# Shifting four attention operand tiles by 64 bytes in on-chip memory

## The chip, the cores and the metric

The kernel runs on one core of one Trainium2 chip. The metric is the device time of one execution in microseconds (us), and the time given for a kernel is the median of its runs. A profiled execution of the kernel before took 845.1 us; the span of its instructions is 843.3 us, and the remaining 1.8 us lie around the span.

## The reference

Two mixers run on the same sequence `x` of 2048 rows by 512 columns in float32, and a gate per row mixes their results.

```python
g = sigmoid((x * gate_w).sum(-1, keepdims=True))
# A: a Fourier layer, the real part of a transform along both axes
a  = x @ dft_hid_re.T;  b = x @ dft_hid_im.T
y  = dft_seq_re @ a - dft_seq_im @ b
# B: attention, 32 heads of 16, each query sees itself and the 255 keys before it
q, k, v = split(x @ wqkv)
p  = softmax(where(0 <= i - j < 256, q @ k.T * 16**-0.5, -1e9))
out = g * y + (1 - g) * ((p @ v) @ wo)
```

## The kernel before, in words

**Two streams on TensorE.** The attention (B) is worked off as 128 steps: four groups of eight heads, and in each group 32 blocks of 64 queries. A step has four parts `p`, each of which holds two heads, stacked as 128 rows of the array. `s_pair` multiplies a block of queries with a window of up to 320 keys and takes the row maximum; `t_pair` runs 19 steps later (`LAG`) and computes the transposed scores with the maximum folded in, for one block of keys and up to 320 queries. Between two such attention matmuls the function `fill` puts dense matmuls of 512 columns: the projections, then the Fourier layer's products over the sequence (`c_part`, line 529). In most of the attention this gives a steady order on TensorE: one attention matmul, two dense ones, one attention matmul, two dense ones. The order of all engines but GpSimd is written out by hand.

**The tiles in question.** `ring[0]` and `ring[1]` hold the queries and the keys of the running groups (128 partitions, four parts of 2048 float32 each). A matmul of `s_pair` or `t_pair` streams a window of a ring past stationary weights, and these weights are a *pad*: `pads[i][b]` is a tile of four parts by 128 columns, in which `make_pad` writes a block of the ring twice, masked by a column `half` of ones and zeros, so that two heads stay apart. There are four pads: `i` is 0 for the queries of `s_pair` and 1 for the keys of `t_pair`, and `b` alternates from step to step. VectorE writes three of the four halves of a step (line 350) and ScalarE one (line 348). So each of the 1024 attention matmuls (512 at line 367, 512 at line 449) has one weight load of 128 columns from a pad.

**Where tiles lie.** A partition of on-chip memory is a row of bytes, and the tiles of the pool `const` lie one behind another in the order in which they are first asked for. Before them stand 1,152 bytes of other things. All sizes per partition are multiples of 128 bytes but those of the small 64-byte columns, so each small tile that is asked for moves everything behind it by 64 bytes. In the kernel before, the order and the start addresses are:

| tile | starts at byte | modulo 128 |
|---|---|---|
| four pads of 2048 bytes | 1152, 3200, 5248, 7296 | 0 |
| two rings of 32768 bytes | 9344, 42112 | 0 |
| `mask`, `ident` | 74880, 76160 | 0 |
| `half` (64 bytes) | 76672 | 0 |
| `vpad` twice | 76736, 78784 | 64 |
| `gl`, `g1`, `g0` (64 bytes each) | 80832, 80896, 80960 | 64, 0, 64 |
| `home` | 81024 | 0 |
| `big`, `hi`, `lo`, `raw`, `ev`, `pt`, `sm` and the rest | from 93376 on | 64 |

The dense matmuls take both operands from `big`, `hi` and `lo`, all at 64 modulo 128. Near the end the products with `wo` (line 922) take both operands from spots in the rings that begin 16 elements, which is 64 bytes, past a multiple of 128 bytes. The pads' memory is used again there: `wo_fetch` and `first_load` put tiles with the pads' tags in it.

Of the kernel before, what the change touches and what calls it, by code (L numbers as in the profile page):

```python
# [7 lines left out]
F32 = mybir.dt.float32  # L8
# [6 lines left out]
P = 128  # L15
# [17 lines left out]
def fnet_window_mix(ctx: ExitStack, tc: tile.TileContext, xT, x, wqk, wv, wr, wi, cr, ci, wo, gw, out):  # L33
    nc = tc.nc

    const = ctx.enter_context(tc.tile_pool(name="const", bufs=1))
# [21 lines left out]
    def f(ap):  # L58
        return ap.bitcast(F32)
# [4 lines left out]
    def mark(e, ins):  # L64
        last[e] = ins.ins

    @contextmanager
    def behind(*engines):
        with ExitStack() as es:
            for e in engines:  # L70
                if e in last:
                    es.enter_context(tc.issue_after(last[e]))
            yield
# [91 lines left out]


    NPAD = 2
    pads = [[const.tile([P, NP, P], F32R, name=f"pad{i}_{b}") for b in range(NPAD)] for i in range(2)]
    ring = [const.tile([P, NP, S], F32R, name=f"ring{i}") for i in range(2)]

    mask = const.tile([P, WIN], F32, name="mask")
# [9 lines left out]
    mark("pool", nc.gpsimd.affine_select(ident[:], f(ident[:]), pattern=[[1, P]], compare_op=OP.is_equal, fill=0.0,  # L181
                                         base=0, channel_multiplier=-1))

    cols = const.tile([P, 16], F32, name="half")
    half, side = cols[:, :2], cols[:, 2:4]
    mrow = cols[:, 4:6]
    for h in range(2):
# [10 lines left out]
    def clear_rows(i, ss):  # L198
        with behind("pool"):
            mark("pool", nc.gpsimd.memset(f(ring[i][96:128, :, ss * 512:(ss + 1) * 512]), 0.0))  # L200
# [4 lines left out]
    for ss in range(4):  # L205
        for i in (1, 0):
            clear_rows(i, ss)
    vpad = [const.tile([P, 4, NP, 32], F32, name=f"vpad{b}") for b in range(2)]

    def clear_pads():  # L210
# [7 lines left out]
                                         mask[96:128, :256].rearrange("r (p c) -> r p c", p=NP),  # L218
                                         AF.Identity, bias=mrow[96:128, h:h + 1], scale=0.0)

    gl = const.tile([P, 16], F32, name="gl")
    g1 = const.tile([P, 16], F32, name="g1")
    g0 = const.tile([P, 16], F32, name="g0")
    gwb = []

# [112 lines left out]
    def make_pad(i, n):  # L338
        if not 0 <= n < NG * NB:
            return  # L340
        t = pads[i][n % NPAD]
        b = n % NB
        with behind(*(("act", "dve") if n < NPAD else ("dve",) if i == 0 and n < 24 else ())):
            for h in range(2):
# [768 lines left out]
```

## Time and profile before

| | value |
|---|---|
| median of 3 runs (lowest, highest) | 845.56 us (845.48, 846.09) |
| profiled execution, its span | 845.1 us, 843.3 us |
| granted TensorE clock | 1.00 |
| TensorE matmul busy (instructions) | 838.5 us, 99% (5310) |
| TensorE weight load busy | 695.8 us, 83% (5310) |
| VectorE busy | 643.8 us, 76% |
| ScalarE busy | 611.1 us, 72% |
| GpSimd busy | 298.8 us, 35% |
| DMA | 161.03 MB, mean 191 GB/s |

A matmul's entry in the profile lasts from the start of its streaming to the modelled end of its results, and the next matmul starts while it is still draining. So a sum of such durations is no sum of time; what one matmul costs is the distance from its start to the next one's start, and this is read from the timeline. The weight load of the next matmul runs while the one before it streams.

### The profile page before, as it was taken

What the parts mean: (1) busy time and instruction counts of PE and PEld (TensorE: products, weight loads), DVE (VectorE), ACT (ScalarE), POOL (GpSimd) and SP (SyncE); (2) the same over time, 40 slices, a digit from 0 to 9 for tenths busy, and PEclk for the clock granted to TensorE, in tenths of its full rate; (3) what the DMA queues carried; (4) which work ended last, traced back from release to release, by engine and by line L of the source; (5) the groups of instructions that cost most, each with busy time, mean ns of one, the idle gap of its engine ahead of it and who ended that gap; (6) DMA issues with size and microseconds to landing.
All of it is one profiled execution on the core that took longest, in us unless ns stands there. A gap on an engine that the chain in (4) does not pass through costs nothing.

```text
span 843.3 us, 17171 instructions
## 1 busy us (share of the span) xinstructions
PE 838.5 (99%) x5310; PEld 695.8 (83%) x5310; DVE 643.8 (76%) x2083; ACT 611.1 (72%) x1832; POOL 298.8 (35%) x606
## 2 busy tenths in 40 slices
PE   9999999999999999999999999999999999999998
PEld 7888888888888888888888887878887878878997
DVE  5588978677979787787877877878987867666874
ACT  6488888878888897787877977867777865553430
POOL 8102333233232233342333243343242357756410
PEclk9999999999999999999999999999999999999999
DMA  8776678485766173534454547979874256455732
GB/s 295 251 227 187 217 243 283 159 259 202 220 222 189 54 232 107 177 120 121 140 160 126 168 153 223 298 214 309 274 216 149 96 179 198 137 192 196 220 133 92
DMA packets 94475, 161.03 MB, mean 191 GB/s; under 512 B 26800, under 2 KB 35504, under 8 KB 94384
## 3 DMA queue, kind: packets, MB, share of 16 engines
q1 hardware_dynamic: 93952, 159.28, 59.1%
q8 instruction: 42, 0.69, 0.3%
q10 hardware_dynamic: 432, 0.66, 0.2%
q14 instruction: 49, 0.40, 0.1%
HBM read 108.27 MB, written 51.64 MB: 190 GB/s over the span
## 4 chain that ended last, share of the span: by engine, by line
PE 99%; DVE 1%; issue 0%; ACT 0%; DVEq 0%; ACTq 0%
PE dc L529 42%; PE dab L304 11%; PE dqk L281 10%; PE t L449 9%; PE s L367 8%; PE o L475 8%; PE dv L304 5%; PE t L922 5%; PE s L269 1%; PE dv L593 0%; PE s L387 0%; DVE pad L350 0%; PE t L559 0%; DVE sm L369 0%; ACT sm L372 0%
## 5 line engine op out<-in xcount | busy, mean ns | idle before, releaser
L529 PE MATMUL dc<-big,hi 128*128 128x512 f32 x1020 | 344.7, 393 | 0.0
L369 DVE CUSTOM_DVE_ANT_0 sm<-s,mask 128x320 f32<-128x320 f32 (+4 forms) x512 | 235.5, 465 | 111.4 <-PE s L367 71.2
L372 ACT ACTIVATE sm<-sm,ml 128x320 f32<-128x320 f32 (+4 forms) x512 | 278.2, 544 | 56.4 <-DVE ml L369 52.1
L450 ACT ACTIVATE pt<-t 128x320 f32<-128x320 f32 (+4 forms) x392 | 159.5, 411 | 83.4 <-PE t L449 78.1
L529 PE MATMUL dc<-big,lo 128*128 128x512 f32 x510 | 200.2, 393 | 0.0
L529 PEld LDWEIGHTS dc<-big,hi 128*128 128x128 f32 x1020 | 179.3, 188 | 21.4
L454 POOL TENSOR_SCALAR_AFFINE_SELECT pt<-pt 128x128 f32<-128x128 f32 x196 | 77.1, 393 | 275.0 <-ACT pt L450 273.7
L449 PE MATMUL t<-ring,pad 128*128 128x320 f32 (+4 forms) x512 | 156.8, 306 | 0.0
L367 PE MATMUL s<-ring,pad 128*128 128x320 f32 (+4 forms) x512 | 154.9, 303 | 0.1
L350 DVE TENSOR_SCALAR pad<-ring,half 96x256 fp32r<-96x256 f32 x384 | 120.0, 359 | 5.4 <-PE t L449 4.9
L449 PEld LDWEIGHTS t<-ring,pad 128*128 128x128 f32 x512 | 96.1, 188 | 30.9 <-issue 8.7
L367 PEld LDWEIGHTS s<-ring,pad 128*128 128x128 f32 x512 | 96.2, 188 | 20.6 <-DVE ml L369 0.7
L529 PEld LDWEIGHTS dc<-big,lo 128*128 128x128 f32 x510 | 95.9, 188 | 12.0
L372 ACT ACTIVATION_READ_ACCUMULATOR sm<-sm,ml 128x1 f32 x512 | 98.1, 192 | 0.0
L588 DVE TENSOR_TENSOR lo<-raw,hi 128x512 fp32r<-128x512 f32 x137 | 94.3, 696 | 2.7 <-ACT hi L588 2.5
L304 PE MATMUL dab<-hi,big 128*128 128x512 f32 x256 | 88.9, 394 | 0.0
L281 PE MATMUL dqk<-big,hi 128*128 128x512 f32 x240 | 85.0, 393 | 0.0
L432 POOL TENSOR_SCALAR vpad<-vr,half 128x256 f32<-128x256 f32 x64 | 62.2, 983 | 62.1 <-PE o L475 29.5
L348 ACT ACTIVATE pad<-ring,half 96x256 fp32r<-96x256 f32 x128 | 66.9, 522 | 0.0
L454 POOL TENSOR_SCALAR_AFFINE_SELECT home<-home 128x128 f32<-128x128 f32 x60 | 33.8, 564 | 90.2 <-ACT home L450 85.7
L458 POOL TENSOR_SCALAR_AFFINE_SELECT pt<-pt 128x128 f32<-128x128 f32 x172 | 62.9, 366 | 0.0
L588 DVE CAST hi<-raw 128x512 fp32r<-128x512 f32 x126 | 54.3, 437 | 11.3 <-PE dc L529 10.6
(122 smaller groups left out, 1034.2 us busy)
## 6 DMA issues: line engine op xcount, KB each, us to landing
qk_scr<-home SPq DMA_DIRECT2D x32, 512.0 KB
ring<-qk_scr SPq DMA_DIRECT2D x32, 512.0 KB
raw<-cr SPq DMA_DIRECT2D x32, 512.0 KB
raw<-ci SPq DMA_DIRECT2D x32, 512.0 KB
r_scr<-ev SPq DMA_DIRECT2D x42, 256.0 KB
ab_scr<-home SPq DMA_DIRECT2D x20, 512.0 KB
big<-ab_scr SPq DMA_DIRECT2D x20, 512.0 KB
ring<-qk_scr SPq DMA_DIRECT2D x32, 256.0 KB
```

The source lines that it names most:

```text
L281: nc.tensor.matmul(ps, w[a][:, c:c + 128], XT[dk, ss][:, b], start=n == 0, stop=n == 11)
L304: nc.tensor.matmul(ps, XT[dk, ss][:, a, c * 128:(c + 1) * 128], wh[b], start=n == 0, stop=n == 11)
L350: mark(f"pad{i}", nc.vector.tensor_scalar(dst, src, half[:96, h:h + 1], None, op0=OP.mult))
L367: nc.tensor.matmul(ps[:, :w], PAD[0, n][:, p], ring[1][:, p, k0:k0 + w], start=True, stop=True)
L369: mark("dve", nc.vector.tensor_tensor_reduce(out=sm[:, :w], in0=ps[:, :w], in1=mask[:, WIN - w:], scale=1.0, scalar=3e38, op0=OP.add, op1= ...
L372: mark("act", nc.scalar.activation(sm[:, :w], sm[:, :w], AF.Exp, bias=nm[:, c], scale=-1.0, accum_out=l[:, c]))
L449: nc.tensor.matmul(ps[:, :w], PAD[1, n][:, p], ring[0][:, p, q0:q0 + w], start=True, stop=True)
L450: nc.scalar.activation(pt[:, p, :w], ps[:, :w], AF.Exp, scale=-1.0)
L454: nc.gpsimd.affine_select(a, a, pattern=[[0, 2], [2, 64]], compare_op=OP.is_ge, fill=0.0, base=1, channel_multiplier=-1)
L475: nc.tensor.matmul(OT[g, sb][32 * p:32 * p + 32, q - sb * 512:e - sb * 512], v2[:, p], pt[:, p, q - q0:e - q0], start=first, stop=kb == 8 ...
L529: nc.tensor.matmul(ps, w[a][:, i % 8 * 128:i % 8 * 128 + 128], ab[SC[i]][:, b], start=i == ends[0] and a + b == 0, stop=i == ends[1] and a ...
L588: return fn(*args)
```

## The change

Three 64-byte tiles are asked for at other places of the program; nothing that any instruction computes changes. `half` now comes ahead of the pads, `gl` between the pads and the rings, and `g1` ahead of `vpad`.

```diff
     NPAD = 2
+    cols = const.tile([P, 16], F32, name="half")
     pads = [[const.tile([P, NP, P], F32R, name=f"pad{i}_{b}") for b in range(NPAD)] for i in range(2)]
+    gl = const.tile([P, 16], F32, name="gl")
     ring = [const.tile([P, NP, S], F32R, name=f"ring{i}") for i in range(2)]
...
-    cols = const.tile([P, 16], F32, name="half")
     half, side = cols[:, :2], cols[:, 2:4]
...
     for ss in range(4):
         for i in (1, 0):
             clear_rows(i, ss)
+    g1 = const.tile([P, 16], F32, name="g1")
     vpad = [const.tile([P, 4, NP, 32], F32, name=f"vpad{b}") for b in range(2)]
...
-    gl = const.tile([P, 16], F32, name="gl")
-    g1 = const.tile([P, 16], F32, name="g1")
     g0 = const.tile([P, 16], F32, name="g0")
```

By the sizes, the pads then start at 1216, 3264, 5312 and 7360, which is 64 modulo 128. The two 64-byte tiles together move the rings by 128 bytes, to 9472 and 42240, which is again 0 modulo 128; `mask`, `ident` and `vpad` move by 128 bytes as well, and `g0`, `home` and all that follows stay where they were.

## The prediction, as put on record

> **What bounds the kernel now.** I read the page first. TensorE is busy for the whole span, at full granted clock, and the chain of waits runs almost only through it.
>
> ```profile
> span 843.3 us, 17171 instructions
> PE 838.5 (99%) x5310; PEld 695.8 (83%) x5310; DVE 643.8 (76%) x2083; ACT 611.1 (72%) x1832; POOL 298.8 (35%) x606
> PE 99%; DVE 1%; issue 0%; ACT 0%; DVEq 0%; ACTq 0%
> ```
>
> So a change shows in the time only if it alters the distance between two matmul starts, or makes TensorE wait. Second view: the waits in front of weight loads, where a late pad would stand.
>
> ```profile
> PEld t L449 <- issue: 8.7, 20, 0.5
> PEld o L475 <- issue: 5.3, 15, 0.4
> ```
>
> These are its two largest entries (total us, times, longest), and no entry names the pad writers at lines 348 and 350. Third, the timeline of TensorE in a steady stretch (start, duration), where each attention matmul is followed by two dense ones:
>
> ```profile
> 362.51 0.31 PE L367 MATMUL s<-ring,pad 128*128 128x320 f32 x1
> 362.65 0.39 PE L529 MATMUL dc<-big,lo 128*128 128x512 f32 x1
> 362.88 0.39 PE L529 MATMUL dc<-big,hi 128*128 128x512 f32 x1
> 363.11 0.31 PE L449 MATMUL t<-ring,pad 128*128 128x320 f32 x1
> ...
> 379.91 0.31 PE L449 MATMUL t<-ring,pad 128*128 128x320 f32 x1
> ...
> 617.14 0.31 PE L449 MATMUL t<-ring,pad 128*128 128x320 f32 x1
> ...
> 641.67 0.31 PE L449 MATMUL t<-ring,pad 128*128 128x320 f32 x1
> ```
>
> From 362.51 to 379.91 the timeline holds 29 such stretches of three matmuls, so one takes 17.40 / 29 = 600 ns. From 617.14 to 641.67 it holds 40, so one takes 24.53 / 40 = 613 ns. The same operands at the same places modulo 128 run in two steady states, 13 ns apart. What sets the state I cannot read.
>
> **The change: what it touches.** Counts come from the groups by shape:
>
> ```profile
> L449 PEld LDWEIGHTS t<-ring,pad 128*128 128x128 f32 x512 | 96.1, 188 | 30.9 <-issue 8.7 <-DVE ml L369 0.8 <-DVE ev L496 0.5
> L367 PEld LDWEIGHTS s<-ring,pad 128*128 128x128 f32 x512 | 96.2, 188 | 20.6 <-DVE ml L369 0.7 <-ACT pt L450 0.4
> L529 PEld LDWEIGHTS dc<-big,hi 128*128 128x128 f32 x1020 | 179.3, 188 | 21.4
> L350 DVE TENSOR_SCALAR pad<-ring,half 96x256 fp32r<-96x256 f32 x384 | 120.0, 359 | 5.4 <-PE t L449 4.9 <-DVE ml L369 0.2
> L348 ACT ACTIVATE pad<-ring,half 96x256 fp32r<-96x256 f32 x128 | 66.9, 522 | 0.0
> ```
>
> No instruction, wait or queue entry is added or removed. 1,024 weight loads read from 64 instead of 0 modulo 128, and 512 writes go there. Rings, mask and `vpad` keep their place modulo 128.
>
> **(a) The load itself.** A pad's load at 0 modulo 128 takes 188 ns and a dense one at 64 takes 188 ns. I take 0 for the load's own time.
>
> **(b) The load beside the streaming matmul.** A pad's load runs beside the dense matmul before the attention matmul. Before, the stream is at 64 and the load at 0; after, both are at 64, as for a dense load beside a dense matmul. What that pairing costs shows late, where three dense matmuls follow each attention matmul:
>
> ```profile
> 717.08 0.31 PE L449 MATMUL t<-ring,pad 128*128 128x320 f32 x1
> 717.23 0.62 PE L529 MATMUL dc<-big,hi 128*128 128x512 f32 x2
> 717.68 0.39 PE L529 MATMUL dc<-big,lo 128*128 128x512 f32 x1
> 717.91 0.31 PE L449 MATMUL t<-ring,pad 128*128 128x320 f32 x1
> ...
> 722.87 0.31 PE L449 MATMUL t<-ring,pad 128*128 128x320 f32 x1
> ```
>
> From 717.08 to 722.87 lie seven stretches, 5.79 / 7 = 827 ns each. Against 600 ns the third dense matmul, whose stream is beside a dense load, costs 827 - 600 = 227 ns. In the rows at 362, the dense matmul beside a pad's load goes from 362.88 to 363.11, 230 ns, in steps of 10. In the seven late stretches it takes on average 224 ns (from 717.68 to 717.91 and six alike), and the two before it 228 each (717.23 to 717.68 and six alike). So the pairing that is coming costs between 3 ns less and 4 ns more than the one that goes, and my value is 0: 227 lies between 224 and 230. Times 1,024 this is -3.1 to +4.1 us, with 0 as forecast.
>
> **A rule beside this.** The Trainium skill, page "SBUF — State Buffer", section "Who interferes with whom", gives TensorE two independent read ports, one for the moving operand and one for weight loads; by it the address of a load cannot touch the stream. The trace agrees to the 4 ns above; it shows only these pairings.
>
> **(c) The attention matmul's own stream** keeps 0 modulo 128, and the load beside it is a dense one, as before: 0. That the class does not tell is seen where both exist in one width, 256:
>
> ```profile
> L922 PE MATMUL t<-ring 128*128 128x256 f32 x312 | 39.9, 283 | 0.0
> L367 PE MATMUL s<-ring,pad 128*128 128x256 f32 x16 | 4.5, 281 | 0.0
> ```
>
> Line 922 has both operands at 64, line 367 both at 0: 283 against 281 ns, which is 2 ns on a modelled duration.
>
> **(d) Writing the pads.** No row writes a pad at 64, so I take the same line or operation with its output in `home` (0) and in a tile at 64:
>
> ```profile
> L450 ACT ACTIVATE pt<-t 128x320 f32<-128x320 f32 x344 | 145.4, 427 | 68.2 <-PE t L449 63.3 <-PE s L367 3.9
> L450 ACT ACTIVATE home<-t 128x320 f32<-128x320 f32 x104 | 44.2, 425 | 7.0 <-PE t L449 5.9 <-POOL home L454 0.4
> L90 DVE TENSOR_TENSOR home<-dqk,home 128x512 fp32r<-128x512 f32 x15 | 10.2, 683 | 1.4 <-ACT home L88 1.4
> L90 DVE TENSOR_TENSOR big<-dab,big 128x512 fp32r<-128x512 f32 x12 | 8.2, 685 | 1.0 <-ACT big L88 1.0
> ```
>
> ScalarE: 427 at 64 and 425 at 0. VectorE: 685 and 683. So a pad write may take 2 ns more: 384 x 2 = 0.8 us on VectorE and 128 x 2 = 0.3 us on ScalarE, over the whole span, hidden under TensorE. The cover:
>
> ```profile
> 300.00:400.00 100.00, 100.00 (x677) 83.24 (x676) 76.68 (x272) 79.73 (x248) 33.22 (x82) 1.00 0.50 151
> ```
>
> The third and fourth busy columns behind the length are VectorE and ScalarE. A step of the attention is eight stretches, 4.8 us, so 100 us hold 21 steps and 63 of VectorE's pad writes; it idles 23.3 us there, 0.37 us for each write. The write would have to double before VectorE became the bound, and then all of the excess would be on the path. I take 0.
>
> **(e) The end.** `wo_fetch` and `first_load` use the pads' memory, so those loads and VectorE's and ScalarE's reads of them move too. (d) prices that at 2 ns an operation, and there are some tens: below 0.1 us.
>
> **The sum.** 0 + 0 + 0 + 0 + 0, so the profiled execution stays at 845.1 us (843.3 of span and 1.8 around it). The median of the three runs is 0.5 us above that, so I put the median at 845.6 us. About 0.2% of it, 1.7 us, is what a measurement of this kernel can tell from no change.
>
> **Rivals.**
>
> *Slower: the like pairing disturbs.* Stream and load at 64 modulo 128 side by side cost more than 64 beside 0, at each of the 1,024 dense matmuls ahead of an attention matmul. For it: the 228 against 224 ns in the late rows. Against: the last dense matmul differs from the others also in what follows it, and its next distance starts from a ring. At 4 ns it adds 4.1 us: 849.7. It shows from 1.7 us / 1,024 = 1.7 ns a load on. Its far form is that each stretch which now takes 600 ns goes to 613: by the starts in the timeline 540 stretches of two dense matmuls keep to 600 or within 3 ns, so 540 x 13.3 = 7.2 us, 852.8.
>
> *Faster: the long state goes.* If the mixture of loads at 0 and at 64 lets the order fall into the 613 ns state, loads all at 64 may keep it out. By the same count 155 stretches of two dense matmuls are one step longer, the forty above among them; 155 x 13.3 = 2.1 us: 843.5. Against: the state comes and goes with the same operands, and the rings stay at 0.
>
> *Much faster: each pad load costs the stream something now.* Between 512 and 320 columns a start-to-start distance falls from 227 to 600 - 2 x 227 = 146 ns, 0.42 ns a column; 512 columns at that rate are 216 ns, so 11 ns of each distance is not streaming. If the 11 ns beside a pad's load went, 1,024 x 11 = 11.3 us would: 834.3. Against: the like pairing, dense beside dense, pays those 11 ns too. The Trainium skill, page "TensorE: Matmul & The Clock Gate", section "Back-to-back issue gap", has the isolated distance as N / 2.4 + 2.5 ns, 216 ns for 512 columns; the trace has 227, so by that rule 11 ns of each are excess that could go.
>
> *The shift does not happen.* If the tiles were packed in another order, pads would stay at 0, and the time is 845.6 as well; this lies in "no change".
>
> **How the numbers follow.** No change within 1.7 us: 0.44, since all rows in (a) to (e) say so, though they resolve 4 ns a load and a load need only move by 1.7. Slower: 0.32, the rival with 849.7 the centre and 852.8 the far end; it has the one row that leans, and two states that a new layout can tip. Faster: 0.24, of which 0.19 for the long state, a little beyond the 1.7 us bound, and 0.05 for the far one. The predicted time is that of no change, whose own range is 843.9 to 847.3. For 8 in 10 I reach down to 842.5, below the long state's 843.5 by the 1 us that other long stretches hold, and up to 851.0, inside the slower rival's far end. Left out are the 0.05 far below and some 0.12 of slower.
>
> **What would show it.** Right: the same instruction counts; pad loads of 188 ns; stretches of 600 ns in the steady rows; pad writes within 2 ns of 359 and 522; no pad writer among the waits. Wrong: stretches of another length, in steps of 13 ns or at the dense matmul ahead of the pad's matmul (slower or faster rival, by the sign); or pad writes far longer, with weight loads waiting for line 350. A different order of instructions would make the whole working void.

## The result, and the profile after

The changed kernel took 855.65 us (median; 855.14 to 855.94), beside 845.52 us (845.10 to 846.09) for the kernel before on the same chip: a ratio of 1.0119 (95% interval 1.0101 to 1.0136). It is slower by 10.1 us. The forecast was no change, 845.6 us, and the range ended at 851.0. The profiled execution took 855.14 us with a span of 853.2 us, at a granted clock of 1.00 as before.

The head of the page after, then busy time by engine and the shares of the chain of waits:

```profile
span 853.2 us, 17171 instructions
PE 848.4 (99%) x5310; PEld 695.7 (82%) x5310; DVE 644.4 (76%) x2083; ACT 612.5 (72%) x1832; POOL 297.0 (35%) x606
PE 99%; DVE 1%; issue 0%; ACT 0%; DVEq 0%; ACTq 0%
```

The counts are the same and so is the bound. TensorE's matmuls are busy 9.9 us longer (848.4 against 838.5), which is all of the 9.9 us by which the span grew. The groups by shape after (count, busy us, mean ns) say which rows did not move:

```profile
L449 PEld LDWEIGHTS t<-ring,pad 128*128 128x128 f32 x512 | 96.1, 188 | 32.6 <-issue 9.1 <-DVE ev L496 0.5 <-DVE ml L369 0.3
L367 PEld LDWEIGHTS s<-ring,pad 128*128 128x128 f32 x512 | 96.1, 188 | 22.6 <-DVE ml L369 0.7 <-ACT pt L450 0.2
L350 DVE TENSOR_SCALAR pad<-ring,half 96x256 fp32r<-96x256 f32 x384 | 119.6, 358 | 6.3 <-PE t L449 5.6 <-DVE ml L369 0.2
L348 ACT ACTIVATE pad<-ring,half 96x256 fp32r<-96x256 f32 x128 | 66.9, 522 | 0.0
L922 PE MATMUL t<-ring 128*128 128x256 f32 x312 | 40.0, 283 | 0.0
```

Pad loads take 188 ns as before, pad writes 358 and 522 ns against 359 and 522. The products with `wo` keep 283 ns; both of their operands lie in the rings and moved together. The two largest entries of the waits in front of weight loads (total us, times, longest) went from 8.7 to 9.1 us and from 5.3 to 5.0, and no writer of a pad is in that view:

```profile
PEld t L449 <- issue: 9.1, 21, 0.5
PEld o L475 <- issue: 5.0, 14, 0.4
```

So no new wait has come up. What did grow are the entries of the dense matmuls; the largest group, before and then after:

```profile
L529 PE MATMUL dc<-big,hi 128*128 128x512 f32 x1020 | 344.7, 393 | 0.0
L529 PE MATMUL dc<-big,hi 128*128 128x512 f32 x1020 | 348.2, 397 | 0.0
```

These lengths reach to a modelled end; the time itself is read from the distances between starts. The timeline of TensorE after, at the place where the kernel before ran 29 stretches of 600 ns:

```profile
366.72 0.31 PE L367 MATMUL s<-ring,pad 128*128 128x320 f32 x1
366.87 0.39 PE L529 MATMUL dc<-big,lo 128*128 128x512 f32 x1
367.10 0.39 PE L529 MATMUL dc<-big,hi 128*128 128x512 f32 x1
367.33 0.31 PE L449 MATMUL t<-ring,pad 128*128 128x320 f32 x1
...
381.44 0.31 PE L367 MATMUL s<-ring,pad 128*128 128x320 f32 x1
```

From 366.72 to 381.44 lie 24 stretches: 14.72 / 24 = 613 ns on average. The trace holds the starts finer than this view prints them, and by them these stretches go round 610, 622 and 608 ns. I matched the 975 stretches with two or three dense matmuls in the two traces one by one, which the same order of instructions allows. The 739 with an attention matmul of 320 columns and two dense ones went from 604.7 to 614.6 ns on average, +7.3 us; the 116 with three dense ones from 839.7 to 855.0, +1.8 us; the narrower ones gave +0.2. That is 9.3 of the 9.9 us. Inside runs of dense matmuls alone the distance (median) stayed at 227 ns. The loss is spread over the whole attention; it is no single place. Within a steady stretch of three, the distance from the attention matmul to the first dense one stayed (146.1 ns before, 146.5 after); those behind the two dense ones rose, from 229.4 to 234.0 and from 227.2 to 232.9.

### The profile page after: what moved, and what is told of

The parts are those of the page before. It is cut to its first block, busy times and chain, and to the rows that moved or that the text cites. A ratio compares the mean times of both kernels' runs of the same rounds, so it can differ in the third digit from the quotient of the medians.

```text
span 853.2 us, 17171 instructions
## 1 busy us (share of the span) xinstructions
PE 848.4 (99%) x5310; PEld 695.7 (82%) x5310; DVE 644.4 (76%) x2083; ACT 612.5 (72%) x1832; POOL 297.0 (35%) x606
## 4 chain that ended last, share of the span: by engine, by line
PE 99%; DVE 1%; issue 0%; ACT 0%; DVEq 0%; ACTq 0%
PE dc L529 42%; PE dab L304 11%; PE dqk L281 10%; PE t L449 9%; PE s L367 8%; PE o L475 8%; PE dv L304 5%; PE t L922 5%; PE s L269 1%; PE dv L593 0%; DVE pad L350 0%; PE s L387 0%; PE t L559 0%; ACT sm L372 0%; DVE sm L369 0%
## 5 line engine op out<-in xcount | busy, mean ns | idle before, releaser
L529 PE MATMUL dc<-big,hi 128*128 128x512 f32 x1020 | 348.2, 397 | 0.0
L529 PE MATMUL dc<-big,lo 128*128 128x512 f32 x510 | 202.8, 398 | 0.0
L454 POOL TENSOR_SCALAR_AFFINE_SELECT home<-home 128x128 f32<-128x128 f32 x60 | 32.0, 534 | 92.9 <-ACT home L450 86.0
L588 DVE CAST hi<-raw 128x512 fp32r<-128x512 f32 x126 | 53.5, 431 | 12.4 <-PE dc L529 10.8
```

Source lines behind the costliest of these rows:

```text
L454: nc.gpsimd.affine_select(a, a, pattern=[[0, 2], [2, 64]], compare_op=OP.is_ge, fill=0.0, base=1, channel_multiplier=-1)
L529: nc.tensor.matmul(ps, w[a][:, i % 8 * 128:i % 8 * 128 + 128], ab[SC[i]][:, b], start=i == ends[0] and a + b == 0, stop=i == ends[1] and a ...
L588: return fn(*args)
```

## The experiments

The prediction reckoned in places modulo 128. The change also moved the rings by 128 bytes, and modulo 256 that is a move. (No view shows an address; the places come from the sizes of the tiles and the order in which they are asked for.) Modulo 256 the places were, before: pads 128, rings 128, dense operands 192; after: pads 192, rings 0, dense 192. A stretch has three pairings of a weight load with the stream that runs beside it, and each is written below as load minus stream, modulo 256: a dense load beside the **ring** stream, a **dense** load beside a dense stream, a **pad** load beside a dense stream. Before they are +64, 0, -64; after -64, 0, 0.

The expectations name theories by letter. A: an attention matmul costs more where its own weights and its own stream differ modulo 128. B: a pad load in the same class as the dense stream beside it disturbs it (the prediction's slower rival). C: it is the rings' place modulo 256. D: it is the place of each weight load against the stream beside it, modulo 256. E: it is absolute places, or other tiles that moved. G: traffic of the other engines is needed for it.

Diffs are against the changed kernel, and short: they show which small tile is asked for where, and so which large one moves (`half`, `gl`, `g1`, `g0` have 64 bytes each). "Stretch" is the mean of the steady stretches with 320 + 512 + 512 columns, from the starts in each trace. Each ratio is to the kernel before, timed in the same round on the same chip; its median was 845.57 to 845.66 us in these rounds.

**Rings alone.** The pads go back; only the rings keep their new place (pairings -64, 0, -64).

```diff
-    cols = const.tile([P, 16], F32, name="half")
     pads = ...
+    cols = const.tile([P, 16], F32, name="half")
     gl = const.tile([P, 16], F32, name="gl")
     ring = ...
```

> Pads back at 0 modulo 128; rings, mask and vpad stay where the change put them, 128 bytes further on than before (rings at 0 instead of 128 modulo 256). If the pads' 64 bytes cost the time (either as weights unlike their own matmul's stream, theory A, or as a load like the dense stream beside it, theory B): 845.5 us, stretches of 600 ns. If the rings' or the mask's new place modulo 256 costs it (theory C): 855.6 us, stretches of 607 to 623 ns.

Measured 856.40 us, ratio 1.0127 (1.0112 to 1.0143), stretch 614.4 ns. Theory B falls: the pad loads are unlike the dense stream again and all of the loss is there. The rings' 128 bytes alone cost 10.8 us, as much as the whole change. Again the distance behind the attention matmul, whose stream is the one that moved, stayed (146.9 ns against 146.1 before); those behind the two dense matmuls rose, from 229.4 to 234.7 and from 227.2 to 232.9.

**Pads alone.** The rings are asked for first and stay at 128 modulo 256; the pads are at 192 (+64, 0, 0).

```diff
+    ring = ...
     cols = const.tile([P, 16], F32, name="half")
     pads = ...
     gl = const.tile([P, 16], F32, name="gl")
-    ring = ...
```

> Rings ahead of the pads, at 128 modulo 256 as in the kernel before; pads at 64 modulo 128. Theories A and B: 855.6 us, since pads and rings differ by 64 as in the changed kernel. Theory C: 845.5 us.

Measured 851.67 us, ratio 1.0073 (1.0057 to 1.0090), stretch 609.8 ns. None of the three theories gave this time. The pads' 64 bytes cost 6.1 us while the rings stay, so C, which is enough for the whole loss above, is not the whole rule. The two costs do not add: 10.8 and 6.1 apart, 10.1 together.

**All large operands at 192.** `gl` comes behind the rings, and the spots of the last products move by 16 elements to keep their class (0, 0, 0).

```diff
-    gl = const.tile([P, 16], F32, name="gl")
     ring = ...
+    gl = const.tile([P, 16], F32, name="gl")
...
-        at_c = m % 4 * S + 16 + 512 * h
+        at_c = m % 4 * S + 512 * h
...
-    COL = 1040, 1552
+    COL = 1024, 1536
```

> Pads and rings both at 64 modulo 128, like the dense operands; the spots of the last products stay at 64. Theory A (an attention matmul is slower when its own weights and its own stream differ modulo 128): they agree again, 845.5 us and 600 ns. Theory B (a weight load is bad beside a stream of the same class modulo 128): now the dense loads beside the attention matmuls' streams are like as well, so at least 855.6 us, up to 866.

Measured 857.32 us, ratio 1.0141 (1.0126 to 1.0156), stretch 618.0 ns: the slowest layout of all, and theory A falls, since each matmul has its own operands in one class. The timeline of this kernel on TensorE, same place:

```profile
366.88 0.31 PE L449 MATMUL t<-ring,pad 128*128 128x320 f32 x1
367.04 0.63 PE L529 MATMUL dc<-big,hi 128*128 128x512 f32 x2
367.50 0.31 PE L367 MATMUL s<-ring,pad 128*128 128x320 f32 x1
...
381.14 0.31 PE L367 MATMUL s<-ring,pad 128*128 128x320 f32 x1
```

From 366.88 to 381.14 lie 23 stretches, 14.26 / 23 = 620 ns each. With load and stream at the same place everywhere, a stretch is 20 ns longer than before.

**Rings at 192 with the pads as before** (0, 0, -64). As in the kernel just shown, but with `half` between pads and rings.

```diff
-    cols = const.tile([P, 16], F32, name="half")
     pads = ...
-    gl = const.tile([P, 16], F32, name="gl")
+    cols = const.tile([P, 16], F32, name="half")
     ring = ...
+    gl = const.tile([P, 16], F32, name="gl")
```

> Pads at 0, rings at 64 modulo 128; the spots of the last products stay at 64. Theory A: weights and stream of the attention matmuls differ, 855.6 us. Theory B: the pad loads are unlike the dense stream beside them, but the dense loads are like the ring stream beside them; about 855.6 us too if both places weigh the same, 845.5 if only the load beside the dense stream counts.

Measured 851.31 us, ratio 1.0066 (1.0051 to 1.0081), stretch 608.9 ns, with 607 the most common length; neither 845.5 nor 855.6, the two values that had been expected. Between this kernel and the last, only the pads' place differs: 6.0 us.

**The same pairings at other places, and a control.** In the first kernel the dense operands come down to 128, where pads and rings are (0, 0, 0 again); in the second pads, rings and dense operands stand as before, and only `mask`, `ident` and `vpad` have moved as in the change.

```diff
# first: half, gl and g1 where the kernel before has them, last spots as above, and
-            e = const.tile([P, 16], F32, name="ge")
+            e = g0
# second:
-    cols = const.tile([P, 16], F32, name="half")
     pads = ...
-    gl = const.tile([P, 16], F32, name="gl")
     ring = ...
+    cols = const.tile([P, 16], F32, name="half")
+    gl = const.tile([P, 16], F32, name="gl")
```

> Pads and rings where they were before; the dense operands and all tiles behind them 64 bytes lower, so that every matmul operand begins at 128 modulo 256 (the spots of the last products too). Theory D (what counts is where a weight load begins against the stream beside it, modulo 256): all differences are 0 as in the kernel with everything at 64, so again about 857 us and stretches of 620 ns, the dense matmuls among themselves at 227 ns. Theory E (the absolute place counts, and 0 modulo 128 is the good class): 845 us or less.

> Pads and rings exactly where they were before; mask, ident, half and vpad 128 bytes further on, as in the changed kernel. Theory D: none of these is streamed or loaded in the stretches, so 845.5 us and 600 ns. Theory E in the form that one of these tiles is the cause: 855 us.

The first took 855.23 us, ratio 1.0115 (1.0100 to 1.0130), and its commonest stretch is again 620 ns, though it moved operands that the change had left alone and left those it moved. Theory D had this kernel at about 857 us, as the other one with these pairings. The second took 846.00 us, ratio 1.0005 (0.9995 to 1.0014). E falls: the other tiles do nothing, and neither a pad nor a ring has to move for the loss.

**Other steps of the ring and of the dense pairing.** Rings at 64 (+128, 0, -64) in the first; dense streams at 128 with dense loads at 192, and pads at 64 (+64, +64, -64), in the second.

```diff
# first: pads, half, gl, g1, rings, g0; last spots as above
# second: rings, half, gl, g1, pads, g0; e = g0; and behind the first tile of big
+    big.tile([P, 16], F32, name="gap", bufs=1)
```

> Pads as before (128 modulo 256), rings 192 bytes further on, at 64 modulo 256, so that a dense load begins 128 beyond the stream of an attention matmul instead of 64. With the load before the dense stream as before (64 short of it), the rings gave 845.5 at +64, 851.3 at 0 and 856.4 at 64 short; theory D has no rule for the fourth place yet: 845 to 856 us, from the two neighbours about 851.

> The tiles big, which the late dense matmuls stream, begin 64 bytes lower and hi and lo stay, so that a dense load begins 64 beyond a dense stream instead of at the same place modulo 256; pads and rings are placed so that their two differences stay as before. Theory D: the distance of two dense matmuls changes from 227 ns, and with it the stretch; the sign is open: a saving of 5 ns on some 1,500 late dense matmuls would give 838 us, a loss of 5 ns 853 us. Theory E: 845.5 us.

Measured 849.06 us, ratio 1.0045 (1.0028 to 1.0061), stretch 606.6; and 852.51 us, ratio 1.0083 (1.0068 to 1.0098), stretch 608.2. In the second the distance inside runs of dense matmuls alone rose from 227 to 233 ns, with no pad or ring in them: the plainest sign that it is load against stream. The three pairings given for this kernel, and for the two further down that move `big`, hold for the matmuls that are lines 281 and 529 in the kernel before; the projections at line 304 load from `big` and stream `hi` and `lo`, so theirs are others, and the kernel's time is a mixture.

**The pads' other places.** With the rings first and as before, the order of all pairings is kept (a control), or the pads stand at 0 (+64, 0, +64), at 64 (+64, 0, +128), or 32 bytes on, at 160 (+64, 0, -32).

```diff
# control:     rings, pads, half, gl
# pads at 0:   rings, half, gl, pads
# pads at 64:  rings, half, gl, g1, pads, g0
# pads at 160: rings, half as [P, 8], pads, gl, a gap of 32 bytes
```

> Rings ahead of the pads, everything at the place modulo 256 that it has in the kernel before (pads and rings at 128, dense operands at 192), mask, ident and vpad as in the changed kernel. Theory D (only the place of a load against the stream beside it, modulo 256, counts): 845.6 us within 0.2%, stretches of 600 ns. If the distance counts in larger units, or the order of the tiles: something else, as the 851.7 us of the kernel with rings first and pads at 192.

> Rings first, at 128 modulo 256 as before; pads at 0 modulo 256, so that a pad's load begins 64 beyond the dense stream beside it (before: 64 short). Theory D: differs from 845.6 us by the fit of this one pairing; both other places tried beside this ring (64 short: 845.6, same: 851.7) leave it open; the dense pairing got slower at 64 beyond (233 against 227 ns), so 848 to 853 us. By 0 modulo 128 being the good class for pads: 845.6.

> Rings first, at 128 modulo 256 as before; pads at 64 modulo 256, the fourth place, so that a pad's load begins 128 beyond the dense stream beside it. Theory D: open, 845 to 853 us. By 64 modulo 128 being the bad class for pads: 851.7 us as with pads at 192.

> Rings first, as before modulo 256; pads at 160 modulo 256, so that a pad's load begins 32 bytes short of the dense stream's place, half way between the good 64 short (845.6 us) and the bad same place (851.7). Theory D with a smooth dependence: 847 to 850 us. If only whole 64-byte lines count, 160 lies in the line of 128 and the time is 845.6 us.

The control took 846.22 us, ratio 1.0005 (0.9996 to 1.0014), although pads and rings had changed places. Pads at 64 took 852.02 (1.0056 to 1.0087), pads at 160 848.98 (1.0025 to 1.0054). Pads at 0 took 844.22 us over ten runs (843.31 to 844.73), ratio 0.9982 (0.9972 to 0.9991): it beats both kernels, by 1.3 and 11.4 us. Theory D had put it at 848 to 853 us, so that guess missed. 619 of its 739 stretches take 600 ns, against 505 before. Where the kernel before had its forty stretches of 613 ns, this kernel's timeline reads:

```profile
617.05 0.31 PE L449 MATMUL t<-ring,pad 128*128 128x320 f32 x1
...
641.65 0.31 PE L367 MATMUL s<-ring,pad 128*128 128x320 f32 x1
```

Between these lie 41 stretches: 24.60 / 41 = 600 ns. The long state is gone there. Beside rings at 128 the pads alone would also fit a period of 128 bytes: 844.2 and 845.6 us at 0 and 128, 852.0 and 851.7 at 64 and 192. What shows that 128 is not enough is the rings.

**Dense streams at other places.** With small tiles between the tiles of `big` and `hi`, dense streams stand at 0 (pairings +64, -64, -64) or at 64 (+64, +128, +64), dense loads at 192.

```diff
# first: rings, half, pads, gl, and in the pool of big, behind its tiles
+    g1, g0, ge = (big.tile([P, 16], F32, name=x, bufs=1) for x in ("g1", "g0", "ge"))
# second: rings, pads, half, gl, and
+    g0, ge = (big.tile([P, 16], F32, name=x, bufs=1) for x in ("g0", "ge"))
# both:
-            e = const.tile([P, 16], F32, name="ge")
+            e = ge
```

> The tiles big begin 192 bytes lower, hi and lo stay, so that a late dense load begins 64 short of the dense stream beside it, as a pad's load does in the kernel before; pads and rings placed so that their differences to their neighbours stay as before. Theory D: the distance of late dense matmuls among themselves changes from 227 ns, and the time with it; if 64 short is the good place for this pairing too, it falls below 227 and the kernel below 845.6 us (3 ns on 1,500 of them: 841); otherwise 850 or more.

> The tiles big 128 bytes lower, hi and lo stay, so that a late dense load begins 128 beyond the dense stream; ring's load 64 beyond as before, pad's load 64 beyond the dense stream as in the fastest kernel so far. Theory D: the distance of late dense matmuls changes from 227; both neighbours gave 233, so 850 to 856 us; below 844 only if this is the better of the two even places.

Measured 854.70 us (1.0086 to 1.0120) and 855.61 us (1.0102 to 1.0132). Dense runs alone went to 233 and 232 ns, so 64 short, where the pads' load stands before, is no good place for a dense load beside a dense stream. In the second the pads and the rings stand, modulo 256, where they stood before.

**TensorE alone.** A kernel of weight loads and matmuls in the order attention, dense, dense, thirty times for each set of pairings, with the other engines idle; nothing of the reference is computed.

> No part of the computation is kept: TensorE alone repeats 30 times the stretch attention matmul (320 columns), dense, dense, for each of the 16 combinations of the ring's and the pad's place modulo 256 against the dense operands, then with the dense load moved, with the pad by 32 bytes, and at last 30 dense matmuls among themselves for each of four places. Theory D (TensorE's own load beside its own stream): the stretches show the kernel's lengths: near 600 ns for the kernel before (ring's load 64 beyond, pad's load 64 short) and for the pad 64 beyond, 608 to 623 for the changed kernel's places (64 short, same), 620 or less for all at the same place, dense among themselves 227 at the same place and 233 at 64 either way. Theory G (other engines' reads and writes of the same memory are needed): all 16 are alike.

The busy times in the stretch that holds the sets (behind the length: PE, PEld, VectorE, ScalarE, GpSimd, clock, DMA share, GB/s):

```profile
23.90:465.00 441.10, 441.10 (x2183) 378.08 (x2182) 0.00 (x0) 0.00 (x0) 0.00 (x0) 1.00 0.00 1
```

G falls: the other engines did nothing, and the lengths came as in the kernel. The mean of the last 24 distances of each set, with the dense pairing at 0, in ns:

| ring pairing | pad 0 | pad +64 | pad +128 | pad -64 |
|---|---|---|---|---|
| 0 | 620.0 | 606.7 | 606.7 | 606.6 |
| +64 | 606.7 | **600.0** | 606.7 | 613.3 (before) |
| +128 | 613.3 | 613.3 | 603.3 | 606.7 |
| -64 | 613.3 (after) | 613.3 | 611.1 | 616.7 |

The kernels with these pairings, by their stretches below 640 ns, stand in the same order, all but the kernel before: 601.0 where the table has 600.0 (pads at 0); 606.6, 608.9, 609.8 and 610.7 where it has 606.6 or 606.7 (rings at 64, rings at 192, pads alone, pads at 64); 613.3 where it has 613.3 (the changed kernel); 614.4 where it has 616.7 (rings alone); 618.0 and 615.0 where it has 620.0. The kernel before has 602.7 against 613.3. The changed kernel's pairings go round 610, 623 and 607 ns here, nearly the 610, 622 and 608 of the kernel itself. A set with the changed kernel's pairings, in the timeline:

```profile
245.14 0.31 PE L52 MATMUL s<-ring,pad 128*128 128x320 f32 x1
245.76 0.31 PE L52 MATMUL s<-ring,pad 128*128 128x320 f32 x1
246.37 0.31 PE L52 MATMUL s<-ring,pad 128*128 128x320 f32 x1
246.99 0.31 PE L52 MATMUL s<-ring,pad 128*128 128x320 f32 x1
```

Dense matmuls alone, thirty in each row, with the load at the same place as the stream, then 64, 128 and 192 bytes past it:

```profile
465.85 7.07 PE L44 MATMUL d<-big,hi 128*128 128x512 f32 x30
472.79 7.24 PE L44 MATMUL d<-big,hi 128*128 128x512 f32 x30
479.89 7.21 PE L44 MATMUL d<-big,hi 128*128 128x512 f32 x30
486.97 7.12 PE L44 MATMUL d<-big,hi 128*128 128x512 f32 x30
```

Against the first row, the second is 0.17 us longer, which over 29 distances is 6 ns each: the 227 and 233 ns of the kernels.

**Why before's pairings gave 600 in the kernel and 613 here.** The same kernel, with eight different first matmuls (64 to 456 columns) ahead of twenty stretches each, for three sets of pairings: the kernel before's, pads at 0, the changed kernel's.

> No part of the computation is kept: TensorE alone, three pairs of places, each entered eight times after a dense matmul of another width (64 to 456 columns), 20 stretches each. If the entry decides the state: at the places of the kernel before (ring's load 64 beyond, pad's 64 short) some of the eight runs settle at 600 and some at 613 ns; at the places of the fastest kernel (both 64 beyond) all or nearly all at 600; at those of the changed kernel (64 short, same) none below 607, mean 613. If the rest of the kernel decides it: 613 in all eight at the places of the kernel before.

The first and last of 18 stretches in the timeline, for the pairings before, then for pads at 0, then for those after:

```profile
86.83 0.31 PE L51 MATMUL s<-ring,pad 128*128 128x320 f32 x1
...
97.63 0.31 PE L51 MATMUL s<-ring,pad 128*128 128x320 f32 x1
...
184.03 0.31 PE L51 MATMUL s<-ring,pad 128*128 128x320 f32 x1
...
194.84 0.31 PE L51 MATMUL s<-ring,pad 128*128 128x320 f32 x1
...
282.52 0.31 PE L51 MATMUL s<-ring,pad 128*128 128x320 f32 x1
283.14 0.31 PE L51 MATMUL s<-ring,pad 128*128 128x320 f32 x1
283.75 0.31 PE L51 MATMUL s<-ring,pad 128*128 128x320 f32 x1
284.38 0.31 PE L51 MATMUL s<-ring,pad 128*128 128x320 f32 x1
...
293.58 0.31 PE L51 MATMUL s<-ring,pad 128*128 128x320 f32 x1
```

10.80 / 18 = 600, 10.81 / 18 = 601 and 11.06 / 18 = 614 ns. Before's pairings came to 600 with all eight first matmuls; one theory had some of them at 613, the other all, so both missed. The pairings after went round 610, 623 and 607 with all eight, and never took 600. So the pairings before have been seen in both states (600 here, 613 in the other small kernel and in part of the real one, there with the same round of 613, 613 and 614 ns), and those after had no steady 600 in either small kernel. What puts the pairings before into 613 was not found.

## Why the prediction was wrong

**What bounds the kernel** was right: the distance between matmul starts set the time. **(a)** and **(d)** were right: loads of 188 ns, pad writes within 1 ns of before, no pad writer among the waits. **(e)** was small as said: behind the last attention matmul the trace is 0.1 us longer.

**(c) failed, and this is the step that made the prediction wrong.** It put 0 for the rings because they kept their class modulo 128. Modulo 256 they went from 128 to 0, and the load beside their stream from +64 to -64. With nothing but that, the kernel lost 10.8 us. The attention matmul's own distance did stay, as (c) said (146.1 against 146.9 ns); the loss came out at the two dense matmuls behind it, for which (c) had no term. The row offered as support, line 922 against line 367 at 256 columns, compared modelled durations and not distances, and could not show it.

**(b) failed as a rule.** It bounded the new pairing between -3.1 and +4.1 us by distances of single matmuls; beside rings that stay, the pads' move cost 6.1 us. Beside the moved rings it cost nothing (856.40 us without it, 855.65 with it), so it is luck that (b)'s error does not show in this change. A price for each pairing is the wrong form: 6.1 and 10.8 us alone are 10.1 together, and a pad place is good or bad only beside a given ring place (in TensorE alone, pad +64 takes 600 at ring +64 and 613 at ring +128). That the two pairings cost the same was read from rows that all held the rings' pairing of +64. Part of its spread was the view's steps of 10 ns: by the finer starts the three late dense matmuls take 228, 227 and 226 ns, not 228, 228 and 224, so the one row that leaned to "slower" hardly leaned.

**The rule beside it.** The Trainium skill, page "SBUF — State Buffer", section "Who interferes with whom", gives TensorE independent read ports for stream and weights. I concluded that the load's address cannot touch the stream, and that the trace agreed to 4 ns. The runs disagree with that conclusion: 227 against 233 ns for dense matmuls alone, and 600 to 620 for a stretch, by address alone and with the other engines idle. The measurement decides; whether it is the ports or something behind them, no run shows.

**The sum** came out 10.1 us short. **The rivals:** "slower" had 0.32 and its far form, 600 going to 613, was nearest: 852.8. The step came in the size described: the 508 stretches of an attention matmul of 320 columns and two dense ones that lay within 3 ns of 600 rose by 13.2 ns each on average, 6.7 us. What the far form left out is the stretches with three dense matmuls, 1.8 us, and others. Its mechanism fell, though: the loss is whole with the pads unlike the dense stream, so that its size came out near is luck. The range stopped at 851.0, inside that far form, and so cut off what happened. "The long state goes" was no effect of this change, but it exists, as a layout: pads at 0 brought 1.3 us, near the 2.1 us worked out for it. "Much faster" came about in no run: the fastest layout took 844.2 us, and no place of the load brought a run of dense matmuls below 227 ns. "The shift does not happen" is out, since the time moved.

**What would show it wrong** was named rightly: stretches of another length, with the counts, the pad loads and the pad writes as before.

**Open.** What inside TensorE or the memory makes the conflict. Which of the pairings does it, since three relations describe a layout and the runs vary places, not one port. Why pairings before have two states. Layouts with equal pairings still differ by up to 2.1 us (857.3 and 855.2), which the pairings do not say. Steps below 64 bytes were tried only at 32. That 256 bytes is the period is not shown for pads and dense operands, since no run has one of them 256 bytes further on. For the rings it fits: their windows step by 256 bytes from block to block, and in the kernel before blocks of even and odd number have the same stretches (602.9 and 602.4 ns at line 367, 602.8 and 602.7 at line 449).

## What to carry to other kernels

Where a run of matmuls sets the time, as here with 320 and 512 columns and a weight load for each, treat the places of weights and streams as one layout: write down load minus stream for every neighbouring pair, modulo 256 bytes at least, and price a move by the length of the whole repeating stretch. Any small tile asked for earlier moves all that lies behind it, so look at what else moved, and to which period, before calling it unmoved. A handful of 64-byte shifts of one tile is cheap to try: here they spread the same instructions over 844.2 to 857.3 us.

## What the runs showed of the hardware

I had not expected that a move of 128 bytes, with the instruction counts unchanged, weight loads still at 188 ns and no new wait, costs 10.8 us in 845.6. Load and stream at the same place are best for dense matmuls of 512 columns among themselves (227 ns against 229 to 233) and worst for the mixed stretch (620 against 600). And the same instructions at the same places can keep one of two lengths, 600 or 613 ns, for tens of stretches.
